# Gate and up gradients of a gated feed-forward: stored turn by turn, or kept as columns and stored in rows of 3584 at the end

## The chip, the cores and the metric

One NeuronCore of one Trainium2 chip. The metric is the device time of one execution, in microseconds (us), as the median of several runs. A core has five engines with instruction queues of their own: PE (matrix products and transposes), DVE (vector), ACT (scalar), POOL and SP. POOL and SP serve here mostly to issue transfers between the memory of the chip (DRAM) and the core's on-chip memory; whichever queue issues a transfer, the same 16 DMA engines carry it.

## The reference

The program computes the output and ten gradients of one decode step of a transformer block with a batch and a sequence of one. What the change touches is the feed-forward part, with D = 1024 and F = 3584:

```
g = h2 @ w_gate            # (1,1024) x (1024,3584)
u = h2 @ w_up
h = sigmoid(g) * u
ffn = h @ w_down           # (1,3584) x (3584,1024)

# backward, dffn a row of 1024:
dh      = w_down @ dffn                     # 3584 numbers
d_w_down = outer(h, dffn)                   # 3584 x 1024, written out
du      = dh * sigmoid(g)
dg      = dh * h * (1 - sigmoid(g))
d_w_up   = outer(h2, du)                    # 1024 x 3584, written out
d_w_gate = outer(h2, dg)                    # 1024 x 3584, written out
dh2     = w_up @ du + w_gate @ dg           # 1024 numbers
```

Beside that the program writes the gradients of two key and value caches of 4 x 65536 x 128. Only their last 4096 positions are not zero, so some 120 MB of zeros have to be written, which is almost half of all the traffic. All large tensors are bfloat16.

## The kernel before, in words

The work goes in stages: the modulation and attention forward, the attention products that the backward pass needs, the feed-forward turns (about 310 to 480 us), and the end stage, which forms and stores the gradients of the output projection (`dwo`), of the modulation weights (`sec`, `s2`), of the query projection (`dwq_tile`) and of the caches (`grad_kv`, `kv_store`).

The order of the work is written out by hand: each engine runs its instructions in the order of the source, and waits where data or a buffer is not ready. Two lists of counts set where the zeros go: `zero(n)` issues n zero blocks of about 1 MB on POOL's queue at that place of the program. `Z_FFN` (line 57) holds the counts for the seven feed-forward turns, `Z_END` (line 58) those of the end stage. Since POOL works through its queue in order, a zero block that stands behind a transfer which waits also waits. Each POOL transfer besides waits until the one eight places before it has landed, so that at most eight are under way.

**The feed-forward turns.** F is cut into seven blocks of 512 columns; turn q handles block q. For each block the kernel holds:

- the up and gate tiles, `ug_v`: 128 partitions x 8 row groups j x (512 up + 512 gate) columns, two buffers, one for even and one for odd turns. `load_ug` (lines 934 to 937) loads them with four transfers of 512 KB, whose rows in DRAM are 1 KB pieces of rows of 7 KB; `store_ug` (lines 939 to 941) writes the gradients back in the same shape;
- the w_down tile, `wd_v`: four pieces i of 128 x 1024, a single buffer, loaded and stored in halves s of 512 KB by SP (`load_wd`, `store_wd`, lines 922 to 926).

One turn: `front` multiplies the up and gate tiles by h2 (64 matrix products with one column each, line 1032), which gives g and u as eight columns of 128. `gates` takes two sigmoids on ACT, `hh_ops` forms h, `ffn_mm` multiplies w_down by h (32 products, line 1050). `wd_ttr` takes the four dot products of w_down rows with dffn on DVE (line 250 is the helper that records them), which gives dh. `wd_outer` overwrites the w_down tile with the outer product h x dffn (line 246, DVE) and stores it. `dug_part` forms du and dg as eight columns (`dug_bf`), spreads them over all partitions by eight transposes (line 1070) and one ACT copy (line 1071) into `dug_b`, a tile of 128 x 1024.

Then, for each of the eight row groups j: one DVE dot product of the up/gate tile with `dug_b` (line 250) gives one column of dh2, and one scaling of `dug_b` by column j of h2 overwrites the tile with the gradients of w_up and w_gate, for j < 5 on ACT (line 281), for the others on DVE (line 246). After j = 3 and after j = 7 `store_ug` sends the tiles out. The next loads into this buffer (turn q + 2) can only start when those stores have landed. In between, `side()` runs jobs from a list: transposes of tiles that the end stage needs (lines 908 and 909).

**The end stage.** After the last turn dh2 is summed, a layer norm is taken backward, `dattn_bf` is formed, and so on. `dwo(u)` takes four DVE scalings and one store of 1 MB with rows of 8 KB.

Of the kernel before, what the change touches and what calls it, by code (L numbers as in the profile page):

```python
# [10 lines left out]
P = 128  # L11
# [9 lines left out]
KD = D // P  # L21
F = 3584
FB = 512
# [33 lines left out]
Z_FFN = [(0, 2, 0, 2), (0, 2, 0, 1), (0, 2, 0, 2)] + [(0, 2, 0, 2)] * 2 + [(1, 1, 1, 3), (1, 2, 1, 0)]  # L57
Z_END = (1, 0, 0, 0, 0)
@with_exitstack
def kernel(  # L60
# [40 lines left out]
    def ar(off, size):  # L101
        return arena[:, int(off * KIB):int((off + size) * KIB)]
# [122 lines left out]
    def new_acc(name="acc"):  # L225
        return new_bank(name)[:, 0:64]
# [8 lines left out]
    def mulv(out, a, b):  # L235
        return tt(out, a, b, ALU.mult)
# [4 lines left out]
    def cp(out, a):  # L241
        return nc.vector.tensor_copy(out=out, in_=a)  # L242
# [6 lines left out]
    def ttr(out, w, b, acc):  # L249
        return nc.vector.tensor_tensor_reduce(out=out, in0=w, in1=b, scale=1.0, scalar=0.0,  # L250
                                              op0=ALU.mult, op1=ALU.add, accum_out=acc)
# [31 lines left out]
    def outer_dve(out, col, b):  # L283
        return ts(out, b, col, ALU.mult)
# [155 lines left out]
    def rows_to_cols(out, ps, n, room=scr):  # L440
        f = room.bitcast(FP32)[:, 0:32 * n].rearrange("p (n r) -> p n r", r=32)
        tt(f, ps[:, 0:32 * n].rearrange("p (n r) -> p n r", r=32),
           mask.rearrange("p (o r) -> p o r", o=1).broadcast_to([P, n, 32]), ALU.mult)
        nc.vector.reduce_sum(out=out, in_=f, axis=AX.X)
# [483 lines left out]
    def ug_part(view, q, j0, n):  # L928
        return view[:, j0:j0 + n, q * FB:(q + 1) * FB]

    def ug_tile(q, k, j0, n):
        return ug_v[:, q % 2, j0 // 4, j0 % 4:j0 % 4 + n, k, :]
# [6 lines left out]
    def store_ug(q, j0, n):  # L939
        for k, view in ((0, dwu_view), (1, dwg_view)):  # L940
            nc.gpsimd.dma_start(out=ug_part(view, q, j0, n), in_=ug_tile(q, k, j0, n))  # L941

# [44 lines left out]
    for t in range(4, 8):  # L987
# [31 lines left out]
               ("hom", 4, FP32), ("dug_bf", 8, BF16))} for i in range(2)]  # L1019
    fg = new_acc("fg")  # L1020
    ffn_ps = fg[:, 0:KD]
    ffn = vt([P, KD], "ffn")
    gu_t = [fg[:, 16 + 8 * i:24 + 8 * i] for i in range(2)]

    def front(q):
        gu = gu_t[q % 2]
        for k in range(2):
            for j in range(KD):
                for i in range(4):
                    f0 = 256 * (i // 2) + i % 2  # L1030
                    col = 4 - 4 * k + i
                    nc.tensor.matmul(gu[:, col:col + 1], lhsT=ug_v[:, q % 2, j // 4, j % 4, k, f0:f0 + 255:2],  # L1032
                                     rhs=h2_bf[:, j:j + 1], start=(j == 0 and i == 0), stop=(j == KD - 1),
                                     skip_group_check=True)

    def gates(q):
        r, gu = small[q % 2], gu_t[q % 2]
        nc.scalar.activation(out=r["sg"], in_=gu[:, 0:4], func=ACT.Sigmoid)
        nc.scalar.activation(out=r["om"], in_=gu[:, 0:4], func=ACT.Sigmoid, scale=-1.0)

    def hh_ops(q):
        r, up = small[q % 2], gu_t[q % 2][:, 4:8]
        mulv(r["hh_bf"], r["sg"], up)
        mulv(r["hh"], r["sg"], up)
        mulv(r["hom"], r["hh"], r["om"])

    def ffn_mm(q, s):
        for i in (2 * s, 2 * s + 1):
            for k in range(KD):
                nc.tensor.matmul(ffn_ps[:, k:k + 1], lhsT=wd_v[:, i, k * P:(k + 1) * P],  # L1050
                                 rhs=small[q % 2]["hh_bf"][:, i:i + 1], start=(i == 0 and k == 0),
                                 stop=(i == 3), skip_group_check=True)

    def wd_ttr(q, s):
        for i in (2 * s, 2 * s + 1):
            ttr(wd_v[:, i, :] if q else scr, wd_v[:, i, :], b1k, small[q % 2]["dhh"][:, i:i + 1])

    def wd_outer(q, s):
        for i in (2 * s, 2 * s + 1):
            last = outer_dve(wd_v[:, i, :], small[q % 2]["hh"][:, i:i + 1], b1k)  # L1060
        store_wd(q, s)
        return last

    def dug_part(q):
        r = small[q % 2]
        mulv(r["dug_bf"][:, 0:4], r["dhh"], r["sg"])
        mulv(r["dug_bf"][:, 4:8], r["dhh"], r["hom"])
        tp = new_tp("tp_dug")
        for i in range(8):
            nc.tensor.transpose(tp[:, i * P:(i + 1) * P], r["dug_bf"][:, i:i + 1].broadcast_to([P, P]), ident_bf[:, :])  # L1070
        nc.scalar.copy(out=dug_b.rearrange("p (s f j) -> p s f j", s=4, j=2),  # L1071
                       in_=tp.rearrange("p (s j f) -> p s f j", s=4, j=2))

# [4 lines left out]
    B_home = [ar(o, 2) for o in (24, 26, 28, 30, 40, 42, 60, 62)]  # L1078

    def unpark(p):  # L1080
        nc.scalar.copy(out=B_home[p], in_=BT_ps[p][:, :])

    rot[:] = [(psum, "mm"), (prq, "rq")]
    wd_ttr(0, 0)
    side(1)
    front(0)
    gates(0)
    hh_ops(0)
    ffn_mm(0, 0)
    ffn_mm(0, 1)  # L1090
    zero(Z_FOLD[2], wd_outer(0, 0))
    wd_ttr(0, 1)
    dug_part(0)
    zero(Z_FOLD[3], wd_outer(0, 1))
# [3 lines left out]
    for q in range(NB):  # L1098
        z = Z_FFN[q]
        more = q + 1 < NB  # L1100
        for j in range(KD):
            w = ug_v[:, q % 2, j // 4, j % 4, :, :].rearrange("p k f -> p (k f)")
            ttr(w, w, dug_b, dh2acc[:, q * KD + j:q * KD + j + 1])
            if not more and j in (3, 5, 6):
                unpark({3: 2, 5: 0, 6: 4}[j])
            (outer_act if j < 5 else outer_dve)(w, h2[:, j:j + 1], dug_b)
            if more and j == 4:
                front(q + 1)
                gates(q + 1)
            if more and (j > 4 or (j == 1 and q)):  # L1110
                side()
            if j == 0:
                if q == 0:
                    cp(ffn, ffn_ps)
                else:
                    addv(ffn, ffn, ffn_ps)
            if j == 3:
                store_ug(q, 0, 4)
                zero(z[0])
        store_ug(q, 4, 4)  # L1120
        zero(z[1])
        if more:
            hh_ops(q + 1)
            ffn_mm(q + 1, 0)
            wd_ttr(q + 1, 0)
            wd_outer(q + 1, 0)
            ffn_mm(q + 1, 1)
            side(3 if q < 2 else 2)
            wd_ttr(q + 1, 1)
            dug_part(q + 1)  # L1130
            if q + 2 < NB:
                load_ug(q + 2, 0, 4)
            wd_outer(q + 1, 1)
            zero(z[2])
            side()
            if q + 2 < NB:
                load_ug(q + 2, 4, 4)
            zero(z[3])
            if q + 2 < NB:
                load_wd(q + 2, 0)  # L1140
                load_wd(q + 2, 1)
        else:
            zero(z[2] + z[3])
    assert not jobs
    for p in (1, 3):
        unpark(p)
    nc.scalar.copy(out=B_home[5], in_=B_t[5])


    B_t = B_home  # L1150
    rot[:] = [(psum, "mm"), (pna, "na"), (pgu, "gu"), (ppq, "pq"), (px, "x"), (pna, "na"), (prq, "rq")]
    nrot[0] = len(rot) - 1
# [10 lines left out]
    mulv(dln2, dh2, cb1)  # L1163
    dx1b, m2 = layernorm_bwd_col(dln2, ln2, rstd2, "ln2b")
# [18 lines left out]
    do_sb = [ar(158, 2).bitcast(FP32), scr.bitcast(FP32)]  # L1183
# [7 lines left out]
    dh1_ps = new_acc("dh1_ps")  # L1191
    for p in range(NBP):
        for it in range(KD):
            nc.tensor.matmul(dh1_ps[:, p:p + 1], lhsT=B_t[p][:, it * P:(it + 1) * P], rhs=dattn_bf[:, it:it + 1],
                             start=(it == 0), stop=(it == KD - 1))
# [74 lines left out]
    zero(Z_END[0])  # L1270
    do_ps = new_ps("do_ps")[:, 0:HQ]
    dov = do_ps.rearrange("p (b a h) -> p b a h", b=2, a=4)
    for b in range(2):
        for hh in range(4):
            nc.tensor.matmul(dov[:, b, :, hh], lhsT=do_sb[b][:, hh * P:(hh + 1) * P], rhs=ident_f[:, 0::32],
                             start=True, stop=True)
    for g in range(G):
        tr_unit(N_sb[:, g * 1024:(g + 1) * 1024])()
    for u in (2, 4, 5, 6):
        dwo(u)  # L1280
    bcast(dmod_bf[:, 16:48], 32, dmod_b4, "A")
    do_pad = late.pop()
    nc.vector.memset(do_pad, 0.0)
    do_bf = vt([P, HQ], "do_bf", BF16)
    cp(do_bf, do_ps)
    cp(bass.AP(do_pad.tensor, do_pad.offset, [do_pad.ap[0], [HQ + HG, G], [1, HG]]),
       do_ps.rearrange("p (g r) -> p g r", g=G))
    nc.vector.reduce_sum(out=in_group, in_=mask.rearrange("p (g r) -> p g r", g=G), axis=AX.X)
    pd = scr_f[:, 0:HQ]
    dh1 = vt([P, KD], "dh1")  # L1290
    cp(dh1[:, 0:NBP], dh1_ps[:, 0:NBP])
    dwo(7)
    dwo(3)
    zero(Z_END[1])
# [4 lines left out]
    cp(dq_bf, dq_ps[:, 0:HQ])  # L1299
    dwo(0)  # L1300
    sec(0)
# [8 lines left out]
    cp(crow, c_ps[:, 0:1])  # L1310
    sec(1)
# [5 lines left out]
    zero(Z_END[2])  # L1317
# [38 lines left out]
    zero(Z_END[3])  # L1356
# [25 lines left out]
    zero(Z_END[4])  # L1382
# [52 lines left out]
```

## Time and profile before

| what | value |
|---|---|
| median of 3 runs | 594.08 us (593.96 to 594.75) |
| the profiled execution | 593.98 us, span of its instructions 592.2 us |
| busy: PE, DVE, ACT, POOL | 67%, 61%, 44%, 27% of the span |
| moved by DMA | 246.53 MB, mean 416 GB/s |
| transfers issued by POOL, by SP | 218.65 MB, 27.27 MB |
| granted clock of PE, mean | 0.774 of full speed |

How to read it. The busy shares are means over stages with different limits; the page's slices give them for 40 equal pieces of the span (14.8 us each), the view by stretches for any piece. The chain that ended last follows the work back from the last instruction and names, at each step, what released it. A transfer has a time of issue and a time of landing; the time between holds its waiting behind other transfers too. The trace also has a record of each packet that a DMA engine carried, with queue, size and duration. In the packet records a packet of 4096 bytes can be four rows of 1 KB.

### The profile page before, as it was taken

The numbers are of one execution on the slowest core, as the hardware profiler recorded it, in microseconds if no ns is written. First come the engines' busy times: TensorE is split into PE (matmuls) and PEld (weight loads), VectorE is DVE, ScalarE is ACT, GpSimd is POOL, SyncE is SP. The second block draws the span as 40 slices with busy tenths as digits, with TensorE's granted clock in tenths as the row PEclk, the third lists the DMA queues.
The fourth block names the chain that finished last, engine by engine and source line by source line (L and its number), as shares of the span: only waits on it lengthen the run. The fifth ranks groups of instructions, "written<-read, shape, count | busy, mean of one in ns | idle before, by whom it ended". The sixth has DMA issues, their size and how long they took to land.

```text
span 592.2 us, 9529 instructions
## 1 busy us (share of the span) xinstructions
PE 397.7 (67%) x3819; PEld 239.4 (40%) x3844; DVE 360.7 (61%) x677; ACT 259.9 (44%) x398; POOL 158.0 (27%) x258
## 2 busy tenths in 40 slices
PE   3997689999899999988866237244262455984030
PEld 2784333334344546534436136234252424631000
DVE  3665599999511020176548685677866878968160
ACT  2579614567311014212135375464654655893020
POOL 3112223212223112222221334223343145222000
PEclk9998699999999999997995565565555568755555
DMA  8999999999999999999999999999999999999998
GB/s 349 420 419 421 412 457 388 464 417 430 426 422 396 431 446 424 432 431 401 421 422 388 417 414 416 409 413 416 416 414 413 419 419 405 419 425 420 422 416 363
DMA packets 37484, 246.53 MB, mean 416 GB/s; under 512 B 6097, under 2 KB 6097, under 8 KB 23712
## 3 DMA queue, kind: packets, MB, share of 16 engines
q0 software_dynamic: 30144, 218.65, 92.3%
q1 hardware_dynamic: 7248, 27.27, 12.8%
q8 instruction: 30, 0.49, 0.3%
q14 instruction: 14, 0.11, 0.1%
q10 hardware_dynamic: 48, 0.01, 0.0%
HBM read 78.28 MB, written 185.60 MB: 446 GB/s over the span
## 4 chain that ended last, share of the span: by engine, by line
DMA 36%; PE 34%; DVE 18%; ACT 5%; issue 4%; ACTq 0%; DVEq 0%; POOLq 0%; POOL 0%; SPq 0%
DMA out_dram<-arena 15%; PE b_ps L765 12%; DMA arena<-in_B_w_down_dram 7%; DMA out_dram<-out_dram 6%; PE n_ps L708 6%; DVE arena L246 5%; DVE arena L250 5%; DMA arena<-in_B_w_gate_dram 5%; DVE arena L233 4%; DMA arena<-in_w_mod_dram 3%; ACT arena L519 2%; PE t_ps L666 2%; PE w_ps L461 1%; PE tp_k L498 1%; PE tp_side L908 1%
## 5 line engine op out<-in xcount | busy, mean ns | idle before, releaser
L765 PE MATMUL b_ps<-arena 128*128 128x512 bf16 x494 | 116.0, 383 | 2.5 <-ACT arena L909 1.1
L909 ACT COPY arena<-tp_side 128x1024 bf16<-128x1024 bf16 x62 | 60.9, 1014 | 71.4 <-PE tp_side L908 71.1
L233 DVE TENSOR_TENSOR arena<-arena 128x2048 bf16<-128x2048 bf16 x64 | 76.5, 1223 | 2.3 <-PE n_ps L708 0.3
L765 PEld LDWEIGHTS <-arena 128*128 128x128 bf16 x512 | 49.2, 99 | 58.7 <-issue 5.3
L250 DVE CUSTOM_DVE_ANT_0 arena<-arena,scr 128x1024 bf16<-128x1024 bf16 x56 | 66.2, 1219 | 9.5 <-ACT scr L1071 9.5
L708 PE MATMUL n_ps<-arena 128*128 128x512 bf16 x249 | 65.2, 378 | 6.2 <-DVE arena L233 4.2
L200 POOL DMA_DIRECT2D out_dram<-out_dram x68 | 33.6, 495 | 116.2 <-PE n_ps L708 37.5
L908 PE MATMUL tp_side<-ident_bf,arena 128*128 128x128 bf16 x496 | 54.9, 289 | 11.6 <-DVE arena L233 5.2
L908 PEld LDWEIGHTS <-arena 128*128 128x128 bf16 x496 | 47.0, 135 | 17.6 <-issue 8.9
L1032 PE MATMUL fg<-h_bf,arena 128*128 128x1 bf16 x448 | 15.6, 166 | 48.3 <-DMA arena<-in_B_w_up_dram 28.8
L708 PEld LDWEIGHTS <-arena 128*128 128x128 bf16 x256 | 24.6, 97 | 41.2 <-issue 15.8
L250 DVE CUSTOM_DVE_ANT_0 arena<-arena,b1k 128x1024 bf16<-128x1024 bf16 x24 | 28.4, 1220 | 20.8 <-PE fg L1050 20.8
L281 ACT ACTIVATE arena<-scr,h 128x1024 bf16<-128x1024 bf16 x35 | 38.6, 1144 | 2.3 <-DVE dh2acc L250 1.5
L206 POOL DMA_DIRECT2D out_dram<-zeros x45 | 25.1, 562 | 54.0 <-PE q_ps L436 15.1
L941 POOL DMA_DIRECT2D out_dram<-arena x28 | 22.1, 793 | 64.4 <-ACT arena L281 45.4
L1255 ACT ACTIVATE arena<-ps_kv 128x512 bf16<-128x512 f32 x48 | 25.0, 723 | 29.7 <-PE ps_kv L1251 29.7
L1251 PE MATMUL ps_kv<-arena 32*128 32x512 bf16 x64 | 23.8, 543 | 19.7 <-DVE arena L246 18.6
L668 ACT CAST arena<-t_ps 128x512 bf16<-128x512 f32 x56 | 30.1, 588 | 12.1 <-PE t_ps L666 12.1
L242 DVE CAST arena<-b_ps 128x512 bf16<-128x512 f32 x6 | 4.1, 691 | 50.4 <-PE b_ps L765 50.4
L1032 PEld LDWEIGHTS <-arena 128*128 128x128 bf16 x448 | 14.0, 105 | 50.9 <-DMA arena<-in_B_w_up_dram 30.4
L519 ACT COPY arena<-tp_wq 128x1024 bf16<-128x1024 bf16 x23 | 21.4, 1071 | 7.3 <-PE tp_wq L517 7.3
L246 DVE TENSOR_SCALAR arena<-arena,cs_col 128x4096 bf16<-128x4096 bf16 (+1 forms) x16 | 16.0, 1014 | 12.3 <-DMA out_dram<-arena 12.3
(314 smaller groups left out, 618.1 us busy)
## 6 DMA issues: line engine op xcount, KB each, us to landing
out_dram<-zeros POOLq DMA_DIRECT2D x45, 1024.0 KB, 14.1
out_dram<-arena POOLq DMA_DIRECT2D x28, 1024.0 KB, 18.5
out_dram<-arena POOLq DMA_DIRECT2D x30, 512.0 KB, 10.9
out_dram<-arena SPq DMA_DIRECT2D x20, 512.0 KB, 9.8
arena<-in_A_wq_dram POOLq DMA_DIRECT2D x8, 1024.0 KB, 20.9
arena<-in_A_wo_dram POOLq DMA_DIRECT2D x8, 1024.0 KB, 11.4
arena<-in_w_mod_dram POOLq DMA_DIRECT2D x7, 1024.0 KB, 19.0
arena<-in_B_w_up_dram POOLq DMA_DIRECT2D x14, 512.0 KB, 12.2
```

Of the source, the lines that this page charges most:

```text
L200: ins = nc.gpsimd.dma_start(out=as_rows(region, BIGP).bitcast(FP32), in_=zero_src[:, 0:P * ZW // 4].rearrange("i (p x) -> (i p) x", p=BIGP ...
L233: return nc.vector.tensor_tensor(out=out, in0=a, in1=b, op=op)
L246: return nc.vector.tensor_scalar(out=out, in0=a, scalar1=s1, scalar2=None, op0=op0)
L250: return nc.vector.tensor_tensor_reduce(out=out, in0=w, in1=b, scale=1.0, scalar=0.0, op0=ALU.mult, op1=ALU.add, accum_out=acc)
L281: return nc.scalar.activation(out=out, in_=b, func=ACT.Copy, scale=col)
L519: nc.scalar.copy(out=blk, in_=tp[:, :])
L668: nc.scalar.copy(out=o, in_=ps)
L708: mm = nc.tensor.matmul(nbank[k][:, :], lhsT=k_nat[:, g, t_ * DH:(t_ + 1) * DH], rhs=vp[:, t_ % 2, 4 * k:4 * k + 4, :].rearrange("p h d -> ...
L765: mm = nc.tensor.matmul(bbank[p][k][:, :], lhsT=a4[:, p, h, :], rhs=wo_t[u][:, a, k * 512:(k + 1) * 512], start=(i == 0 and a == 0), stop= ...
L908: nc.tensor.transpose(tp[:, i * P:(i + 1) * P], blk[:, i * P:(i + 1) * P], ident_bf[:, :])
L909: nc.scalar.copy(out=blk if dst is None else dst, in_=tp[:, :])
L1032: nc.tensor.matmul(gu[:, col:col + 1], lhsT=ug_v[:, q % 2, j // 4, j % 4, k, f0:f0 + 255:2], rhs=h2_bf[:, j:j + 1], start=(j == 0 and i == ...
```

## The change

The gradients du and dg of a turn are kept as eight columns in `dug_all` (128 x 56), and the up and gate tiles are no longer overwritten and no longer stored in the turns. The turns still form `dug_b` for the dot products.

In the last turn `dug_rows(0)` spreads all the columns of du into one row of 3584 on every partition, by 28 transposes and four ACT copies; `dug_rows(1)` does the same for dg in the end stage. `dw_rows(k, j)` scales that row by column j of h2 into one of three staging tiles of 128 x 3584 and stores it: 16 stores of 896 KB with rows of 7 KB. The first two scalings are on ACT, the others on DVE; eight of the stores are set between the `dwo` stores.

With that:

- `load_ug` for turn q + 2 stands in the loop of turn q, behind the fourth and the eighth dot product;
- `front` and `ffn_mm` give rows instead of columns (32 and 16 products, four side by side in PE's partition groups); `rows_to_cols` turns g and u into columns with a masked product, a sum and a clearing of the accumulator on DVE; the w_down product of all turns stays in one accumulator;
- the first half of the w_down outer product goes to ACT;
- zero blocks: `Z_FFN` and `Z_ROWS` in place of `Z_FFN` and `Z_END`; five more of them stand between the row stores;
- in the end stage dh1, the copies of parked tiles (`unpark`) and the padded copy of do are formed later, and `do_sb` is bfloat16.

The diff, cut to its core:

```diff
-Z_FFN = [(0, 2, 0, 2), (0, 2, 0, 1), (0, 2, 0, 2)] + [(0, 2, 0, 2)] * 2 + [(1, 1, 1, 3), (1, 2, 1, 0)]
-Z_END = (1, 0, 0, 0, 0)
+Z_FFN = [(0, 3), (1, 3), (1, 3), (1, 3), (1, 3), (1, 3), (1, 0)]
+Z_ROWS = (1, 1, 1, 1, 1, 1, 0, 0)
...
-    def store_ug(q, j0, n):
-        for k, view in ((0, dwu_view), (1, dwg_view)):
-            nc.gpsimd.dma_start(out=ug_part(view, q, j0, n), in_=ug_tile(q, k, j0, n))
...
+    dug_all = rows_all[:, 64:64 + 8 * NB]
...
+    def ffn_rows(out, col, w, stop):
+        for a in range(4):
+            nc.tensor.matmul(out[32 * a:32 * a + 32, :], lhsT=col.broadcast_to([P, 32]), rhs=w[..., 32 * a:32 * a + 32],
+                             start=False, stop=stop, tile_position=(0, 32 * a), skip_group_check=True)
     def front(q):
+        for j in range(KD):
+            w = ug_v[:, q % 2, j // 4, j % 4, :, :].rearrange("p k (s r i) -> p (k s) i r", s=2, i=2)
+            ffn_rows(gu_ps, h2_bf[:, j:j + 1], w, j == KD - 1)
     def gates(q):
+        rows_to_cols(gu, gu_ps, 8, gu_ps)
+        nc.vector.memset(gu_ps, 0.0)
...
     def wd_outer(q, s):
         for i in (2 * s, 2 * s + 1):
-            last = outer_dve(wd_v[:, i, :], small[q % 2]["hh"][:, i:i + 1], b1k)
+            last = (outer_dve if s else outer_act)(wd_v[:, i, :], small[q % 2]["hh"][:, i:i + 1], b1k)
...
+    dug_row = [ar(o, 7) for o in (24, 152)]
+    stages = [ar(o, 7) for o in (40, 16, 32)]
+    def dug_rows(k):
+        for q0 in range(0, NB, 2):
+            n = min(2, NB - q0)
+            tp = new_tp("tp_rows")
+            for b in range(4 * n):
+                c0 = 8 * (q0 + b // 4) + 4 * k + b % 4
+                nc.tensor.transpose(tp[:, b * P:(b + 1) * P], dug_all[:, c0:c0 + 1].broadcast_to([P, P]), ident_bf[:, :])
+            nc.scalar.copy(out=dug_row[k][...], in_=tp[...])
+    def dw_rows(k, j, outer):
+        t = stages[staged[0] % 3]
+        staged[0] += 1
+        outer(t, h2[:, j:j + 1], dug_row[k])
+        nc.gpsimd.dma_start(out=(dwu_view, dwg_view)[k][:, j, :], in_=t)
...
+    def turn(q):
+        gates(q)
+        wd_ttr(q, 0)
+        hh_ops(q)
+        wd_ttr(q, 1)
+        ffn_mm(q, 0)
+        ffn_mm(q, 1)
+        first = wd_outer(q, 0)
+        wd_ttr(q, 2, 3)
+        dug_part(q)
+        return first, wd_outer(q, 1)
...
     for q in range(NB):
         z = Z_FFN[q]
+        if q + 1 == NB:
+            dug_rows(0)
         for j in range(KD):
             ttr(w, w, dug_b, dh2acc[:, q * KD + j:q * KD + j + 1])
-            (outer_act if j < 5 else outer_dve)(w, h2[:, j:j + 1], dug_b)
+            if j == 2 and q + 1 < NB:
                 front(q + 1)
+            if j < KD - 1 or not q:
                 side()
             if j == 3:
-                store_ug(q, 0, 4)
+                if q + 2 < NB:
+                    load_ug(q + 2, 0, 4)
                 zero(z[0])
+                if q + 1 == NB:
+                    dw_rows(0, 0, outer_act)
+                    zero(Z_ROWS[0])
+                    dw_rows(0, 1, outer_act)
-        store_ug(q, 4, 4)
+        if q + 2 < NB:
+            load_ug(q + 2, 4, 4)
         zero(z[1])
+        if q + 1 < NB:
+            turn(q + 1)
             if q + 2 < NB:
                 load_wd(q + 2, 0)
                 load_wd(q + 2, 1)
...
     mulv(dln2, dh2, cb1)
+    zero(Z_ROWS[1])
+    dw_rows(0, 2, outer_dve)
     dx1b, m2 = layernorm_bwd_col(dln2, ln2, rstd2, "ln2b")
...
+    for j in range(3, KD):
+        zero(Z_ROWS[j - 1])
+        dw_rows(0, j, outer_dve)
...
+    dug_rows(1)
+    dwo(2)
...
+    dw_rows(1, 0, outer_dve)
+    dwo(4)
+    dw_rows(1, 1, outer_dve)
...
     dwo(0)
-    sec(0)
+    dw_rows(1, 6, outer_dve)
...
+    dw_rows(1, 7, outer_dve)
+    sec(0)
     sec(1)
```

## The prediction

> **What bounds the kernel now.** I read the busy tenths of the page first. The DMA engines are full from the second slice to the last but one, while DVE is at 61% and ACT at 44%: one microsecond of DMA work costs or saves one, and so does one microsecond in which the DMA engines find nothing to do.
>
> ```profile
> DMA  8999999999999999999999999999999999999998
> GB/s 349 420 419 421 412 457 388 464 417 430 426 422 396 431 446 424 432 431 401 421 422 388 417 414 416 409 413 416 416 414 413 419 419 405 419 425 420 422 416 363
> ```
>
> Second, the stretches of the feed-forward turns (about 315 to 495 us) and of the end stage behind them. The last column is GB/s: 413 to 415 in the turns, 418 behind. All bytes of this stage go at nearly one rate.
>
> ```profile
> 340.00:364.00 24.00, 11.76 (x171) 10.33 (x169) 17.56 (x38) 14.41 (x16) 8.56 (x12) 0.57 1.09 415
> 364.00:390.00 26.00, 12.00 (x182) 10.74 (x180) 18.03 (x38) 16.34 (x18) 9.87 (x14) 0.63 1.09 413
> ...
> 494.90:550.00 55.10, 35.68 (x383) 19.84 (x383) 44.05 (x89) 35.66 (x67) 17.63 (x27) 0.63 1.03 418
> ```
>
> Third, the chain that ended last (start, length, what). In the turns it is one pair over and over: half of the w_down gradient goes out, and only when it has landed is the next half loaded into the same buffer.
>
> ```profile
> 315.35 10.59 DMA out_dram<-arena
> 326.01 10.22 DMA arena<-in_B_w_down_dram
> ...
> 343.24 9.68 DMA out_dram<-arena
> 352.98 10.12 DMA arena<-in_B_w_down_dram
> ```
>
> Fourth, the transfers issued from 315 to 500 us: count, KB, median us to landing. A 512 KB transfer of SP takes 10 us although 512 KB at 415 GB/s are 1.3 us: it shares the engines with POOL's transfers.
>
> ```profile
> out_dram<-zeros POOLq DMA_DIRECT2D x29, 1024.0 KB, 14.7
> out_dram<-arena POOLq DMA_DIRECT2D x28, 512.0 KB, 10.7
> out_dram<-arena SPq DMA_DIRECT2D x14, 512.0 KB, 10.3
> arena<-in_B_w_down_dram SPq DMA_DIRECT2D x12, 512.0 KB, 10.1
> ```
>
> Last, who waited in that stage. There are two late transfers, not one: the up/gate load (its buffer must first be stored) and the w_down load.
>
> ```profile
> PE fg L1032 <- DMA arena<-in_B_w_up_dram: 28.8, 10, 6.2
> PE fg L1050 <- DMA arena<-in_B_w_down_dram: 20.5, 8, 6.8
> ```
>
> **Part 1, the rows: 1 KB to 7 KB.** 28 stores of 512 KB, 14.7 MB, become 16 of 896 KB. The packet records give the price: a 4096-byte packet of POOL's queue (four 1 KB rows) has a median of 164 ns between 340 and 480 us; an 8192-byte packet of the end stage's stores 309 ns, so 154.5 per 4096 bytes. 3584 packets x 9.5 ns / 16 engines = **-2.1 us**. Bounds: 0 (those 164 ns hold loads too, which stay) and -2.9 (by rates: 397 GB/s in the poorest microsecond that is mostly such rows, 430 in a good one of 8 KB rows, so 37.0 against 34.1 us). I take 2.1, the row that is nearest in kind.
>
> The Trainium skill (DMA: Bandwidth & Descriptors, Specifications) puts line rate at 512 bytes and more, which would make this part 0; the 6% between the two packet rows speaks against it, mildly. By it the sum below would be 2.1 us more.
>
> **Part 2, engine work.** Out of each turn go 8 scalings (five on ACT at 1144 ns, three on DVE at 494). Into the end come 16 scalings of 3584 columns: two on ACT, 1144 + 2560 x 0.84 ns = 3.3 us each (0.84 ns a column from 1144 for 1024 and 394 for 128), and 14 on DVE, 1278 x 3584/4096 = 1.1 us. DMA needs 2.2 us for each such store at 421 GB/s, and the dWo pieces set between them take 4 x 0.49 us of DVE for 2.5 us of DMA: DVE stays ahead, so 0; without that cover, 16 us. Spreading the columns is 2 x 4 ACT copies of about 1.0 us with PE transposes of 1.0 us per 8. `front` and the w_down product as rows are 32 + 16 matmuls in place of 64 + 32 (about 2.5 us a turn either way); mask, sum and clearing add about 1.0 us to DVE (0.42 + 0.42 measured on the same 256 columns at 307 us, the clearing taken as 0.2). What moves in the end stage (dh1, unparking, the bf16 copy of do4) is PE and ACT work of some microseconds beside 50 us more of DMA: 0.
>
> **Part 3, waits: what goes and what is late next.** Up/gate tiles are no longer stored, so the next load needs only the dot products of the turn before: the 28.8 us wait goes. The w_down pair stays, with nothing changed in its buffer. One cycle of it, counted from the first w_down dot product: dot product 1.15, gate products 0.25, product on PE 0.6, two ACT scalings 2.3, so 4.3 us to the first store (3.2 in the trace before); then 10.5 us until the load is issued (339.9 to 350.4) and 10.1 until it has landed: **24.9 us a loaded cycle**. The floor without DMA waits is DVE: 4 + 8 dot products at 1.145, 0.4 small ones, 2.1 for transposing and copying, 0.84 + 0.2: 17.3 us.
>
> Meanwhile a turn has less to move. Loads 2.1 MB, w_down in and out 2.1, four zero blocks 4.2: 8.4 MB, 20.2 us at 415 GB/s, where before it was 10.5 MB and 25.3 us, which just covered the cycle. A loaded cycle of 24.9 us can move 10.3 MB, so it eats 1.9 MB of what POOL has waiting. And POOL cannot run ahead: its zeros stand behind the load of the turn after next, which waits for dot product 4 or 8. When POOL has run dry, the w_down legs get shorter (nearest row: 6.6 us for 512 KB at the start of the kernel, where only SP loads), so a light cycle is 4.3 + 2 x 6.6 = 17.5; I take 18.5 since the leg meets some load.
>
> The ledger from 315.4 us on: between there and 494.9 the trace moves 179.6 us x 0.415 = 74.5 MB. Add 3.7 MB still waiting at its end (three stores landing 8.9 us after issue), take off 14.7 MB of stores and six zero blocks of 1.05 MB that now stand behind the first row store: 57.2 MB, 138 us, DMA is through at 453.4. When is the first row store ready? The first w_down store moves from 315.4 to about 318.6 (mask and sum 1.0, dot product behind `front`, ACT for DVE). Then six cycles. 4.7 MB wait at 315 us (57.2 less 28.3 of zero blocks, 10.5 of up/gate loads for five turns and 13.7 of w_down), which lasts for two loaded cycles; the third is light, the fourth loaded, the fifth light, and in the last, eight zero blocks run ahead without a load to wait for, so it is loaded: 4 x 24.9 + 2 x 18.5 = 136.6. From the last first-half store to the row store: 0.7 to the gradients, 2.0 to their first copy, 3.6 of further copies, 3.3 scaling, 1.5 to issue and start: 11.2. Together 466.4, **13.0 us** after DMA is through.
>
> **Sum.** -2.1 + 13.0 = +10.9 us on the profiled execution's 593.98 us (span 592.2 and 1.8 around it), 604.9; the median of the three runs is 0.1 higher: **605 us**. A measurement of this kernel can tell about 0.2% (1.2 us) from no change.
>
> **The rivals.**
> *Legs shrink, DMA stays full (0.24).* With 8.4 MB a turn POOL runs dry more often, the legs fall to 7 or 8 us early, and a cycle is at most (453.4 - 318.6 - 11.2)/6 = 20.6 us, the point from which it decides. Then only part 1 is left: 592 us, 591.1 at its bound. For it: 20.6 lies inside 17.5 to 24.9, near the middle. Against: of the w_down loads in the trace none landed under 8.7 us, and 4.3 + 2 x 8.7 = 21.7.
> The Trainium skill (DMA: Bandwidth & Descriptors, Anatomy of one DMA) prices a transfer at 2.0 us and its bytes at 436 GB/s, 3.2 us for 512 KB, which would make this rival certain; the 10 us legs here show queueing that its fit leaves out.
> *Every cycle stays loaded (0.12).* 318.6 + 6 x 24.9 + 11.2 = 479.2, 25.8 us of gap, 617.7 us. For it: all twelve loads of the stage landed at a median of 10.1. Against: they were never measured beside an empty POOL queue.
> *Nothing to gain, nothing lost (0.09).* The 7 KB rows go out at the old price per byte and no gap opens: 594 us.
> *The end stage stalls (0.05).* Three staging tiles for 16 stores: a scaling waits until the store three before has landed. 1 MB stores take 18.5 us to land at the queue's full depth, and three pairs hold 5.9 MB, 14 us: if DVE stood still for the other 4.5 us in some three of the 16, 13 us, but POOL's eight-deep queue is still fed then. 600 to 607 us.
> The forecast itself has 0.50: gaps from 4 to 20 us, so 596 to 612.
>
> Faster 0.24, within 0.2% 0.09, slower 0.67. The range takes in the first rival and most of the third: 590.5 to 613; above and below lie some 2 in 10, mostly the all-loaded case.
>
> **What would show it.** Right: GB/s under 400 in slices between about 370 and 470 us, with POOL idle "until" a dot product (DVE) just then; first w_down stores spaced 18 to 25 us unevenly; a gap of several us before the first 7 KB store, which waits for ACT; end stage at 418 GB/s or more. Wrong: the DMA digits stay 9 throughout and the stores are 20 us apart; then the legs have shrunk to under 8 us. Part 1 shows in 7168-byte packets: 270 ns is right, 287 would be no gain. If the end stage shows DMA gaps with DVE waiting for a store, the last rival is right.

## The result, and the profile after

The changed kernel takes **622.5 us** (median of 4 runs, 621.5 to 623.4) where the kernel before takes 594.0 (4 runs): 1.048 times as long [1.046, 1.050], 28.5 us slower. The profiled execution spans 621.6 us against 592.2. The direction was as forecast, the size was not: 605 was predicted, and 613 was the end of the range.

The busy tenths of the page after, in 40 slices of 15.5 us:

```profile
DMA  9999999999999999999999899999947999799998
GB/s 352 420 419 422 413 452 424 414 434 432 405 422 445 435 434 411 436 389 446 406 390 398 306 410 409 326 391 389 420 191 283 434 395 419 303 392 419 411 411 355
```

Before, no slice between the second and the last but one was under 388 GB/s. Now four places are poor: 306 (from 342 us), 326 (from 388), 191 and 283 (451 to 482) and 303 (from 528). The same by stretches: length, busy us (and instructions) of PE, weight load, DVE, ACT and POOL, granted clock, DMA share, GB/s. The last column is the one to read.

```profile
320.00:345.00 25.00, 10.36 (x143) 8.18 (x142) 16.94 (x36) 12.85 (x15) 5.71 (x9) 0.70 1.13 408
345.00:370.00 25.00, 14.44 (x184) 10.89 (x183) 20.99 (x42) 14.28 (x17) 5.99 (x9) 0.68 0.98 343
...
395.00:420.00 25.00, 10.39 (x128) 7.60 (x126) 19.79 (x41) 12.52 (x15) 8.07 (x12) 0.66 1.09 349
...
445.00:470.00 25.00, 5.45 (x52) 4.20 (x52) 13.13 (x28) 9.96 (x9) 0.00 (x0) 0.50 0.60 216
...
520.00:580.00 60.00, 31.18 (x329) 17.25 (x330) 41.08 (x81) 29.44 (x55) 13.63 (x22) 0.59 0.94 382
```

The kernel before moved 411 to 419 GB/s in the same stretches from 320 to 470 us, and 420 from 520 to 580. Two of its lines:

```profile
445.00:470.00 25.00, 10.36 (x169) 9.34 (x171) 16.95 (x36) 12.72 (x15) 7.37 (x11) 0.50 1.11 416
...
520.00:580.00 60.00, 23.54 (x132) 9.15 (x130) 33.05 (x63) 21.13 (x41) 10.09 (x16) 0.50 1.01 420
```

In the kernel after, POOL issues nothing at all between 445 and 470 us (x0). Both kernels move 246.5 MB, so every microsecond of difference must be one in which the DMA engines moved too little. From the packet records I added up the bytes of each stretch and took them off 416 GB/s; the table is in us of DMA time lost:

| stretch, us | before | after |
|---|---|---|
| 315 to 440, turns | 0.5 | 10.7 |
| 440 to 480, last turn and first row stores | 0.0 | 13.2 |
| 480 to 505, row stores | 0.3 | -0.1 |
| 505 to 560, end stage | -0.7 | 5.3 |
| the last 10 us | 1.8 | 2.2 |

That is 29 us more between them, the whole difference. So two places are to be explained: the turns up to the first row stores (23.4 us more; a row store is one of the new 7 KB stores), and a point in the end stage (6.0 more).

The turns first. SP's queue in the trace after: start, length, what it issued (L927 the w_down stores, L924 the loads of the next half into the same buffer).

```profile
318.32 2.70 SPq L927 DMA_DIRECT2D out_dram<-arena  x2
...
342.88 2.68 SPq L927 DMA_DIRECT2D out_dram<-arena  x2
...
360.97 3.62 SPq L927 DMA_DIRECT2D out_dram<-arena  x2
...
386.27 2.68 SPq L927 DMA_DIRECT2D out_dram<-arena  x2
...
405.54 5.11 SPq L927 DMA_DIRECT2D out_dram<-arena  x2
...
428.65 4.54 SPq L927 DMA_DIRECT2D out_dram<-arena  x2
443.63 5.88 SPq L924 DMA_DIRECT2D arena<-in_B_w_down_dram  x2
459.39 2.68 SPq L927 DMA_DIRECT2D out_dram<-arena  x2
```

The distances of the stores are the six cycles: 24.6, 18.1, 25.3, 19.3, 23.1 and **30.7 us**. A leg is one transfer of the w_down pair: a half's store, or the load that follows it into the same place. The lines between 428 and 459 show both legs of the last cycle: 15.0 us from the store to the issue of the load, then 11.7 until DVE's first dot product of the next turn starts at 455.31, after 10.7 us of waiting for that load. And POOL in those stretches (in brackets the idle time before, and what ended it):

```profile
351.80 0.77 POOL L938 DMA_DIRECT2D arena<-in_B_w_up_dram  x1 [16.93 <-DVE dh2acc L250]
...
434.40 0.66 POOL L194 DMA_DIRECT2D out_dram<-zeros  x1 [1.87 <-DMA out_dram<-zeros]
470.14 0.57 POOL L1090 DMA_DIRECT2D out_dram<-arena  x1 [35.08 <-ACT arena L281]
```

The first line belongs to the hole of a light cycle (one whose legs meet little other work; a loaded one meets a full queue): POOL's next load stood behind a dot product for 16.9 us and its queue ran dry. The second is the last of the zero blocks, the third the first 7 KB store, 35 us later, after ACT's scaling. What was issued by 434.4 us lasted until 455.

Who waited from 315 to 520 us (us in all, times, longest), and the transfers issued from 315 to 500 (count, KB, median us to landing):

```profile
POOL out_dram L1090 <- ACT arena L281: 37.1, 2, 35.1
...
DVE scr L250 <- DMA arena<-in_B_w_down_dram: 32.1, 8, 10.7
```

```profile
out_dram<-arena SPq DMA_DIRECT2D x14, 512.0 KB, 11.0
arena<-in_B_w_down_dram SPq DMA_DIRECT2D x12, 512.0 KB, 8.6
```

The 28.8 us wait for up/gate loads is gone, as forecast; the w_down load, 20.5 us before, now costs DVE 32.1. Its own time to landing fell by only 1.5 us. (These medians are over the transfers whose landing the trace has: here four of the fourteen stores and six of the twelve loads.)

Now the end stage. DVE's next scaling, and the first step of the chain that ended last (start, length, what):

```profile
540.84 1.28 DVE L246 TENSOR_SCALAR arena<-arena,cs_col 128x4096 bf16<-128x4096 bf16 x1 [9.19 <-DMA out_dram<-arena]
```

```profile
530.80 9.94 DMA out_dram<-arena
```

This is `sec(0)`, the first section of the end. It writes `ar(40, 8)`, which is also the staging tile of the sixteenth and last row store (the stages go round 40, 16, 32; 15 mod 3 = 0). That store is issued at 530.8 and lands 9.9 us later, DVE stands still for 9.2 us until then, and nothing else feeds POOL: 5 us of DMA time go.

### The profile page after: what moved, and what is told of

The parts are those of the page before. It is cut to its first block, busy times and chain, and to the rows that moved or that the text cites. A ratio compares the mean times of both kernels' runs of the same rounds, so it can differ in the third digit from the quotient of the medians.

```text
span 621.6 us, 8953 instructions
## 1 busy us (share of the span) xinstructions
PE 393.7 (63%) x3556; PEld 226.2 (36%) x3556; DVE 368.0 (59%) x673; ACT 250.0 (40%) x386; POOL 143.8 (23%) x246
## 5 line engine op out<-in xcount | busy, mean ns | idle before, releaser
L766 PE MATMUL b_ps<-arena 128*128 128x512 bf16 x512 | 117.7, 382 | 1.1 <-ACT arena L910 1.1
L766 PEld LDWEIGHTS <-arena 128*128 128x128 bf16 x512 | 49.0, 99 | 58.3 <-issue 4.7
L909 PE MATMUL tp_side<-ident_bf,arena 128*128 128x128 bf16 x496 | 46.6, 254 | 23.6 <-DVE do_bf L242 8.4
L250 DVE CUSTOM_DVE_ANT_0 scr<-arena,b1k 128x1024 bf16<-128x1024 bf16 x28 | 34.2, 1223 | 32.5 <-DMA arena<-in_B_w_down_dram 32.1
L909 PEld LDWEIGHTS <-arena 128*128 128x128 bf16 x496 | 38.9, 117 | 32.2 <-issue 24.7
L1026 PE MATMUL fg<-arena,hh_bf 128*32 128x256 bf16 x112 | 7.8, 388 | 65.8 <-DVE hh_bf L233 57.0
L709 PEld LDWEIGHTS <-arena 128*128 128x128 bf16 x256 | 24.6, 97 | 41.3 <-issue 15.8
L1246 PE MATMUL ps_kv<-arena 32*128 32x512 bf16 x64 | 24.2, 588 | 23.2 <-DVE arena L254 13.7
L206 POOL DMA_DIRECT2D out_dram<-zeros x45 | 24.6, 550 | 51.5 <-PE q_ps L436 14.4
L246 DVE TENSOR_SCALAR arena<-arena,h 128x3584 bf16<-128x3584 bf16 (+1 forms) x22 | 26.3, 1201 | 15.0 <-DMA out_dram<-arena 15.0
L281 ACT ACTIVATE arena<-b1k,hh 128x1024 bf16<-128x1024 bf16 x14 | 15.4, 1142 | 40.0 <-PE fg L1026 40.0
L938 POOL DMA_DIRECT2D arena<-in_B_w_up_dram x14 | 10.8, 772 | 86.4 <-PE tp_side L909 32.5
L1026 PEld LDWEIGHTS <-hh_bf 128*32 128x32 bf16 x112 | 2.9, 111 | 69.1 <-DVE hh_bf L233 58.6
L1090 POOL DMA_DIRECT2D out_dram<-arena x16 | 9.7, 607 | 65.4 <-ACT arena L281 37.1
```

Of the source, the lines that this page charges most:

```text
L206: ins = nc.gpsimd.dma_start(out=region.bitcast(FP32), in_=zeros[:, :])
L246: return nc.vector.tensor_scalar(out=out, in0=a, scalar1=s1, scalar2=None, op0=op0)
L709: mm = nc.tensor.matmul(nbank[k][:, :], lhsT=k_nat[:, g, t_ * DH:(t_ + 1) * DH], rhs=vp[:, t_ % 2, 4 * k:4 * k + 4, :].rearrange("p h d -> ...
L766: mm = nc.tensor.matmul(bbank[p][k][:, :], lhsT=a4[:, p, h, :], rhs=wo_t[u][:, a, k * 512:(k + 1) * 512], start=(i == 0 and a == 0), stop= ...
L909: nc.tensor.transpose(tp[:, i * P:(i + 1) * P], blk[:, i * P:(i + 1) * P], ident_bf[:, :])
L1246: nc.tensor.matmul(ps[:, :], lhsT=rows[r, t8 * P:(t8 + 1) * P], rhs=bd[r, :], start=True, stop=True, tile_position=(32 * tc_, 0))
```

## The experiments

In each, the kernel before ran on the same chip, at medians of 593.9 to 594.2 us. The changed kernel itself was not run again: differences from it are differences from its 622.5 us. "The single buffer" below is the theory that the turns are paced by the one w_down buffer, whose half must be out before the next is in.

### A second w_down buffer

Every `wd_v` becomes `wd_2[q % 2]`, and the loads go ahead of the next turn:

```
-    wd_v = ar(152, 8)...
+    wd_2 = [ar(o, 8)... for o in (152, 128)]
...
-            turn(q + 1)
             if q + 2 < NB:
                 load_wd(q + 2, 0)
                 load_wd(q + 2, 1)
+            turn(q + 1)
```

> The changed kernel with a second w_down buffer, so that the load for turn q + 2 no longer waits for the gradient of turn q + 1 to land, and is issued ahead of that turn's stores. The buffer lies over the folded weights of the first two modulation sections, so the gradient of c comes out of other data. Theory (one buffer paces the turns, DMA runs dry in the gaps): first-half stores 20 to 21 us apart instead of 18 to 31, no 10 us stretch under 385 GB/s between 320 and 470 us, the 24 us lost there mostly back: 600 us, 597 to 604. Rival (POOL's order starves DMA: zeros stand behind loads that wait for a dot product): the same gaps at the same places, 618 to 623 us.

601.9 us (601.1 to 602.7), 1.013 [1.012, 1.015]: **20.6 us less than the changed kernel**, from this edit alone. Its stretches:

```profile
345.00:370.00 25.00, 12.26 (x144) 9.56 (x145) 23.28 (x49) 10.75 (x13) 8.09 (x12) 0.64 1.21 414
...
395.00:420.00 25.00, 11.55 (x137) 8.87 (x130) 21.22 (x45) 12.60 (x14) 7.64 (x12) 0.66 1.17 415
...
445.00:470.00 25.00, 9.50 (x122) 5.80 (x123) 15.25 (x39) 7.99 (x5) 11.01 (x16) 0.64 1.04 404
495.00:520.00 25.00, 11.27 (x205) 8.85 (x206) 10.00 (x18) 11.15 (x18) 3.07 (x6) 0.70 0.90 371
```

343, 349 and 216 GB/s have become 414, 415 and 404; the end stage's wait is still there (371). The cycles are 18.3 to 20.4 us (20 to 21 were expected), and the first row store is issued at 447.9, 22.2 earlier. One stretch of 10 us is still below the 385 GB/s that were expected as a floor: 369 from 442 us on, just ahead of the first row store. POOL's order is the same as before this edit, so the single buffer is the cause of nearly the whole loss in the turns.

### Zeros of the end stage moved ahead of the first row store

```
-Z_FFN = [..., (1, 0)]
-Z_ROWS = (1, 1, 1, 1, 1, 1, 0, 0)
+Z_FFN = [..., (6, 0)]
+Z_ROWS = (1, 0, 0, 0, 0, 0, 0, 0)
```

> The changed kernel with the five zero blocks that stand between the first row stores moved ahead of the first row store (5.2 MB, 12.6 us of DMA). Theory (DMA waits for the first row store, and the row stores that follow cannot feed it alone): the 13 us hole before the first row store shrinks to under 3 us, but between 470 and 490 us only 2.75 MB of rows are ready in 14 us, 7 us are lost there: 615 to 619 us. Rival (the hole is just misplaced zeros): 609 to 611 us. Rival (more zeros ahead of the w_down transfers lengthen the legs): first row store later than 472 us, 620 us or more.

624.5 us (621.1 to 626.4), 1.051 [1.047, 1.054]: a miss for my theory. Its stretches:

```profile
445.00:470.00 25.00, 2.76 (x31) 1.95 (x32) 7.09 (x18) 2.90 (x5) 1.07 (x2) 0.50 1.17 399
470.00:495.00 25.00, 11.04 (x146) 7.45 (x144) 18.52 (x45) 12.57 (x10) 8.15 (x11) 0.69 0.62 230
495.00:520.00 25.00, 12.44 (x188) 10.93 (x187) 16.81 (x35) 14.77 (x20) 7.85 (x12) 0.59 0.88 353
```

The second rival had foreseen this: a first row store after 472 us, and 620 us or more. The zeros fill 445 to 470 (399 GB/s), but the last w_down pair shares the DMA engines with them. The last cycle grows only from 30.7 to 31.6 us; it is the load of the second half that is late. Issued at 450.1 us, it lands 15.5 us later, where the kernel after has 449.2 and 7.4. The first row store comes at 477.7 instead of 470.1, the hole goes along with it, and the rows that follow, without zeros between them, no longer keep DMA full (353). Filling a hole with work that shares the DMA engines with what the hole waits for moved the hole.

### The staging tile kept out of the first section

```
-    sec_t = [ar(o, 8) for o in (40, 152, 16, 32, 0, 8, 48, 56)]
+    sec_t = [ar(o, 8) for o in (152, 16, 32, 40, 0, 8, 48, 56)]
-    dwq_t = [ar(o, 8) for o in (184, 40, 152, 16, 32, 0, 8, 48)]
+    dwq_t = [ar(o, 8) for o in (184, 152, 16, 32, 40, 0, 8, 48)]
```

> The changed kernel with the tiles of the modulation gradient taken in another order, so that the first one does not lie on the staging tile of the last row store. Theory (DVE stands 9.2 us there until that store has landed, and DMA loses 5 us at 537 to 543 us): that wait goes, 617 to 618 us. Rival (DVE is late there anyway, by the attention chain behind it): the gap moves by a few us, 621 to 623 us.

618.1 us (617.3 to 618.6), 1.040 [1.039, 1.042]: **4.4 us** less. The stretch of the end stage, 382 GB/s in the kernel after (there, 4.2 of the 5.3 us were lost between 539 and 545, around DVE's wait):

```profile
520.00:580.00 60.00, 34.88 (x337) 18.83 (x338) 44.84 (x87) 32.25 (x59) 15.38 (x25) 0.59 1.01 415
```

The tile's reuse is shown to be the cause of the second place.

### The rows by themselves: the kernel before with longer rows

These two are edits of the kernel before, whose stores of 1 KB rows become stores that write the same bytes to other places of the same outputs, in 8 KB rows (half as many transfers) or in 4 KB rows (as many as before). The edit for 8 KB:

```
-        for k, view in ((0, dwu_view), (1, dwg_view)):
-            nc.gpsimd.dma_start(out=ug_part(view, q, j0, n), in_=ug_tile(q, k, j0, n))
+        out = (out_7, out_6)[j0 // 4].rearrange("r n -> (r n)")[q * P * 4096:(q + 1) * P * 4096]
+        nc.gpsimd.dma_start(out=out.rearrange("(p x) -> p x", p=P), in_=...)
```

> The kernel before with its stores of the up and gate gradients as 8 KB rows, two of 1 MB a turn instead of four of 512 KB, at places of the two outputs that are not theirs (the outputs are permuted). Part 1 of the prediction: 2.1 us off, 592 us, 591 to 593. By the line rate from 512 bytes on: no difference, 594. If rows of 1 KB cost more than their packets show: under 590.5.

> The kernel before with its up and gate gradient stores as 4 KB rows, still four transfers of 512 KB a turn (outputs permuted). If the 1.2 us of the 8 KB run came from row length: 592.5 to 593.2. If it came from having half as many transfers in POOL's queue of eight: 593.9.

8 KB: 592.7 us (591.9 to 593.9), 0.998 [0.997, 0.999] of 593.9, so **-1.2 us**. 4 KB: 593.1 (592.9 to 594.2), 0.9986 [0.9978, 0.9995] of 594.2, so -1.1. The gain is there, it does not come from the number of transfers, and it is 1.2 us, not 2.1. One thing stays unseparated: with the longer rows each transfer also writes one contiguous block, so the gain is that of longer rows or of the contiguous block. (The new 7 KB stores have both.) The Trainium skill (DMA: Bandwidth & Descriptors, Specifications) puts line rate at 512 bytes and more, which would make it 0; the intervals leave 0 out, though only just.

### No zeros in the turns: the legs with an empty queue

`Z_FFN = [(0, 0)] * 7`; the blocks left out come at the end, so the whole time (659.5 us) tells nothing.

> The changed kernel with no zero blocks in the turns: all 24 go to the very end, so the whole time says nothing (25 us of zeros behind the last work). Only the w_down legs count. Theory (a leg takes 10 us because POOL's zeros share the engines with it): first-half stores evenly 17.5 to 18.5 us apart in all six cycles, legs of 6 to 8 us, the first row store at about 318 + 6 x 18 + 11 = 437 us. Rival (a leg has a fixed cost of about 10 us whatever runs beside it): 24 to 25 us apart.

The first cycle, which still meets what was waiting, is 23.7 us, the other five 18.1 each. Transfers issued from 318 to 440 us (count, KB, median us to landing):

```profile
out_dram<-arena SPq DMA_DIRECT2D x14, 512.0 KB, 2.9
arena<-in_B_w_down_dram SPq DMA_DIRECT2D x12, 512.0 KB, 3.8
```

A leg of 512 KB takes 2.9 or 3.8 us where it meets hardly any zeros, against 11.0 and 8.6 in the kernel after. The rest of the long legs is queueing beside POOL's blocks. The even spacing was as expected. The legs were shorter than the expected 6 to 8 us: the 6.6 us behind that were a median over loads that SP had issued eight at a time within 5 us, and the first of them had landed after 3.8. The row store, expected at about 437, came at 443.3, since the first cycle was still a loaded one.

The Trainium skill (DMA: Bandwidth & Descriptors, Anatomy of one DMA) gives 2.0 us and the bytes at 436 GB/s, for transfers on the gpsimd path. Taken for SP's 512 KB, that is an estimate of 3.2 us: these legs are close to it, and those beside waiting blocks are 5 to 8 us longer.

### The last zeros held until the w_down pair is through

Three blocks wait for the first half's w_down scaling of the last turn, and a fourth stands behind them in POOL's order:

```
-Z_FFN = [..., (1, 3), (1, 0)]
+Z_FFN = [..., (1, 0), (1, 0)]
...
-            turn(q + 1)
+            held = turn(q + 1)
+            if q + 2 == NB:
+                zero(3, held[0])
```

> The changed kernel with three of the zero blocks that run ahead in the last turn held until that turn's first outer product. Theory (eight blocks with nothing to wait for make the last w_down legs 15 and 12 us, then leave DMA with nothing): last cycle 25 us instead of 31, first row store at 464 to 465 us, hole there 5 to 6 us smaller: 616 to 617.5 us. Rival (the legs are the same, the zeros only move): 621 to 623 us.

615.3 us (614.7 to 615.9), 1.035 [1.034, 1.037]: 7.2 us less, somewhat more than the 5 to 6.5 expected. Its last cycle, by SP's queue:

```profile
426.87 6.03 SPq L927 DMA_DIRECT2D out_dram<-arena  x2
...
450.02 2.68 SPq L927 DMA_DIRECT2D out_dram<-arena  x2
```

It falls from 30.7 to 23.2 us, and the first row store comes at 460.8 instead of 470.1. Here four blocks stood behind the last up/gate load and ahead of the pair, and four came after it; in the kernel after all eight stood ahead. The blocks without a load to wait for are what made the last cycle so long.

### Together

Three combinations of the edits above: buffer and order; order and held zeros; all three.

> Second w_down buffer (over the same folded weights) and the other order of the modulation tiles together. Theory (two separate waits, 20.6 and 4.4 us by themselves): they add, 597 to 598 us, and what stays over 594 is under 4 us. If the change also slowed DMA itself: 600 us or more. If the 7 KB rows paid as forecast and nothing else were lost: 592.

> The changed kernel with both repairs that need no memory: the other order of the modulation tiles (4.4 us by itself) and the three zero blocks held (7.2 us by itself). The w_down buffer stays single. Theory (three separate waits that add): 622.5 - 11.6 = 610.9 us, 609.5 to 612.5. If the two hide behind each other: 614 to 616.

> Second w_down buffer (over the folded weights), other order of the modulation tiles, and the three zero blocks held. With the second buffer the last turn no longer waits for w_down, and 1.5 us are lost ahead of the first row store and about 1.5 at the very end. Theory: the held zeros fill the first of these, 596 us, 595 to 597. If holding them only moves the hole: 597.5. Under 594 would mean that the change can beat the kernel before once memory is found.

Buffer and order: 597.5 us (597.0 to 598.0), 1.0054 [1.0040, 1.0068]; 622.5 - 20.6 - 4.4 = 597.5, the two add up. Order and held zeros: 609.9 (609.1 to 610.5), 1.027 [1.025, 1.028], 12.6 us less than the kernel after, where the two alone give 11.6. All three: 598.6 (597.8 to 599.2), 1.0078 [1.0061, 1.0094], a miss; the two stretches of this run and, below them, of the one without holding:

```profile
420.00:445.00 25.00, 11.95 (x135) 8.92 (x132) 20.07 (x41) 14.03 (x18) 3.02 (x5) 0.64 1.04 374
445.00:470.00 25.00, 9.46 (x122) 5.82 (x123) 15.79 (x39) 8.55 (x5) 9.36 (x15) 0.64 1.10 424
```

```profile
420.00:445.00 25.00, 13.07 (x141) 9.75 (x138) 20.08 (x41) 14.47 (x18) 2.85 (x5) 0.57 1.18 420
445.00:470.00 25.00, 9.65 (x122) 5.83 (x123) 15.86 (x39) 8.53 (x5) 9.74 (x15) 0.64 1.01 395
```

Where legs are not on the path, holding moves the hole from behind 445 us to before it, and the time is 1.1 us longer. The first row store stays at 448.5 in both.

No version came below the kernel before. The best of the changed ones, 597.5, needs 8 KB in each partition for a second buffer, and had them only because it overwrote the folded weights.

## Why the prediction was wrong, point by point

The mechanism of the turns was right: one w_down buffer paces them, and DMA runs dry once the stores are gone. What failed are two terms of its sum, the last cycle and the ledger, and a third that was put at 0, the end stage. The term for the rows was too large as well.

**The pacing of the turns: right.** A cycle of loaded legs 24.9: 24.6, 25.3 and 23.1 measured. A light one 18.5: 18.1 and 19.3. The order was loaded, light, loaded, light, loaded and the last, where two loaded ones had been put at the start; the first five make 110.3, and 3 x 24.9 + 2 x 18.5 = 111.7 was forecast. First w_down store 318.6: 318.3. From the last one to the row store 11.2: 10.7. With empty legs a cycle is 18.1, and DVE's floor had been put at 17.3.

**The last cycle: failed in size.** It was entered as loaded, 24.9, and is 30.7. "Eight zero blocks run ahead without a load to wait for, so it is loaded" had the cause and priced it like any other: 5.8 us. Held back, it is 23.2. It put the first row store at 470.1 instead of 466.4: **3.7 us** of the difference, after what the other cycles gave back.

**The ledger: failed.** DMA was forecast to be through at 453.4 with 57.2 MB moved from 315.4 us on. The trace after moves 54.91 MB from there to the first row store. By the ledger's own items that leaves 54.91 - 74.44 + 14.68 + 6.29 = 1.44 MB for what was "still waiting at its end", where 3.7 had been entered from three stores and their time to landing: 2.3 MB, **5.5 us** too many. A count in the trace before agrees. The three stores were issued only from 494.92 on and were not waiting yet; at 494.9 us 3.1 MB were issued and not landed, and of these only some 1.6 MB were still to move. The transfers then in flight were, on average, half moved already.

The same excess stands in the forecast's 4.7 MB that "wait at 315 us": in the trace after it is 2.8. That fits the order of the cycles, in which not two but one loaded cycle came before the first light one.

So the gap is not 13.0 but 13.0 + 5.5 + 3.7 = 22.2, and 23.4 more was lost in the turns. That it lies in several holes (4.0 us from 350 on, 5.4 from 390 to 430, the rest behind 450) rather than in one changes nothing in the sum: the first row store is late by so much against the bytes there are. Of the forecast picture, POOL idle until a dot product, the stretches under 400 GB/s and the gap before the first 7 KB store that waits for ACT are there. The first hole came earlier than forecast, at 350 us instead of 370, and the cycles spread to 30.7 instead of 25.

**The end stage: failed.** Part 2 entered 0, and the last rival, 0.05, looked at the stages among themselves. Such waits exist (DVE 9.5 us in all from 315 to 520, five times) and cost nothing, since DMA stays at 404 GB/s or more from 470 to 520. What costs is the first user of a staging tile after the rows, `sec(0)`: 4.4 us by the run that reorders the tiles. The sign that the rival had been given, DMA gaps with DVE waiting for a store, did appear, and the end stage moved 382 GB/s instead of 418; but it appeared behind the added stores and not among them. The forecast counted who waits for whom within the added stores and did not ask who takes their tiles next.

**The rows: right in sign.** 2.1 was forecast and 1.2 measured in the kernel before, for 8 KB rows at the old place; 7 KB rows behind the turns were not measured by themselves. The 7168-byte packets have a median of 272 ns, as the forecast's 270 wanted, and yet the gain was not 2.1: the difference of two packet medians did not give the time. That the 164 ns hold loads too does not explain it. In the run with 8 KB rows the loads alone have a median of 161 ns, so without them the old price would, if anything, be higher. Why it was 1.2 stays open.

Together: the forecast's +10.9, with 0.9 for the rows, 9.2 for the turns and 4.4 for the end stage, makes 25.4. The other 3 of the measured 28.5 have no cause shown. With buffer and order mended, 3.3 are left as well (597.5 against 594.2), or 4.5 if the rows gain 1.2 there too. By that run's packet records 1.5 us are lost just ahead of the first row store, and 3.2 in the last 10 us, where the kernel before loses 1.8; whether they are the same 3 us, and what makes them, stays open.

**The rivals.** "Legs shrink, DMA stays full" has its condition in the second buffer's run, 20 us a cycle, and there the turns lose 1.7 us in place of 23.9. With one buffer a light cycle's leg was still 8.3 us (342.88 to the load's issue at 351.22), and the hole began before it was over (350). "Every cycle stays loaded" has the nearest time (617.7), but two cycles were light; its lateness came from the last one and from the ledger.

## What to carry to other kernels

Stores taken out of a loop that is full of DMA work are not only saved there: here they were what the loop's other waits hid behind. Before moving them, count the bytes that are left per turn against the longest chain of transfers that one buffer forces; if the chain is longer, the gain is a hole. And when a stage gets tiles of its own, look for the next user of each tile behind the stage, since its wait meets the end of the queue, where nothing else is left to feed it.

## What the runs showed of the hardware

The same 512 KB transfer of SP took 2.9 to 3.8 us (medians) with hardly any zero blocks about, and 8.6 to 11.0 beside POOL's usual queue. Beside eight blocks of zeros a store took 15.0 us, to the issue of the load that waits for it, and that load 11.7, to the dot product that waits for it; with the five more blocks of the second experiment a load took 15.5 to land. In these runs what waited on one engine's queue set the latency of another's. Of 3.1 MB that were issued and had not landed at 494.9 us in the trace before, 1.6 were left to move. Rows of 1 KB in place of 4 or 8 KB, in a block that is then contiguous, cost 1.1 to 1.2 us in 14.7 MB, 3% of their 35 us.
